# A convolution's first products as two half-width column tiles, copied by one instruction each

## The chip, the cores and the metric

The kernel runs on one core of a Trainium2 chip. The metric is the device time of one execution in microseconds; several executions are given by their median. A profiled execution carries a trace: every instruction with its start, its duration and what released it, every transfer, and the clock that TensorE was granted.

The engines are named as in the profile: PE is TensorE's products, PEld its weight loads, DVE is VectorE, ACT is ScalarE, POOL is GpSimd, and SP issues transfers.

## The reference

The program is a chain of three layers. `x` has 4 batches of 5696 rows and 128 columns, all in fp32.

```python
# layer 1: a causal convolution along the sequence, by FFT of twice the length
Xf = np.fft.rfft(x, n=2*S, axis=1); Hf = np.fft.rfft(h, n=2*S, axis=0)
y = np.fft.irfft(Xf * Hf[None], n=2*S, axis=1)[:, :S]
# layer 2: 8 experts, each takes N/8 rows in the order of their logits, relu(x @ w1) @ w2
# layer 3: 8 experts, each row goes to its best one, times its softmax weight
```

The change is in layer 1 alone. Layers 2 and 3 need all of its output.

## The kernel before, in words

**The convolution as small products.** The sequence of 5696 is 89 x 64. A transform along the 89 is a product with a fixed matrix `F` of 89 x 178 (89 cosines and 89 sines, padded to 96 rows), a transform along the 64 uses one 128 x 128 matrix `EE` per frequency, and the way back uses the transposes and a matrix `G`. All of it is in fp32, and a product of fp32 operands stands in the trace as two weight loads and two passes.

**The first products (`s1`, lines 77 to 94).** The input of one batch lies as 96 partitions (the 89, padded) by 128 `d` by 64. `s1` fetches it in four pieces `g` of 32 `d` into a ring of four buffers `XB` (line 81, issued by SP) and works a piece in four groups `q` of 8 `d`. In a group, each of four products takes the data of two `d` (96 x 128) as weights and streams `F`: the result has 128 partitions, the 64 of the first `d` above the 64 of the second, and 178 columns, cosines ahead of sines. The four results fill 356 columns in each of two banks of a PSUM tile; there are four such tiles, of two banks each, and they are all of PSUM.

The convolution wants something else in SBUF: `A` of 128 partitions (64 cosine, 64 sine) by 89 frequencies by 256 columns, of which one holds one `d` of one batch. So four copies follow, each of 64 partitions and 356 elements: for the first and the second `d` of the pairs, the cosines by ACT and the sines by DVE (line 93). The frequency is the innermost of what a copy writes, with a step of 1 KB between its elements.

**What stands around it.** `s1` runs five times. First for the filter `h`; then for batch 0 in turn with `s2h`, which takes the filter through its second transform (line 106), copies it (line 108) and stores it to `Hd` in DRAM (line 109); one group of `s1` goes with two steps of `s2h`. Then for batch 1. The second transform of these two batches (`s2`, from line 125) needs all of `A` and begins after the last copy; `s3` (line 161) ends the pair and hands rows to the routing. Then `s1` runs for batches 2 and 3, with a step of the routing's search (`head.step`: lines 337 to 406, among them two-column products in line 346) after each group, and `s2` and `s3` follow for that pair. Each stage is in the same instruction streams as the ones around it, in the order that the program gives.

**The order and its limits.** Every engine works its instructions in order. A product needs its piece of `XB` and a free PSUM tile; a copy needs its products; a tile is free when its copies have read it. SP issues the loads of `XB` in order too: a load waits for the products that read the buffer before, and behind the last pieces of `x` stand the matrices `EE` (line 118) and the stored filter (line 122) that `s2` needs.

Of the kernel before, what the change touches and what calls it, by code (L numbers as in the profile page):

```python
# [17 lines left out]
AF = mybir.ActivationFunctionType  # L18
# [30 lines left out]
def conv(tc,nc,a,yrow,LG,head):  # L49

    ctx=contextlib.ExitStack()
    with ctx:
# [6 lines left out]
        F=cp.tile([96,178],F32,name="F"); nc.sync.dma_start(F,a['F'])  # L59
# [5 lines left out]
        A=cp.tile([128,89,256],F32,name="A")  # L65
# [6 lines left out]
        def buf():  # L72
            nx[0]+=1; return XB[nx[0]%4]
        def work(nm): return wk.tile([128,1024],F32,name=nm)
        def apart(i,mine,other):
            tc.declare_no_dep(i.ins,group=other,reason='other columns of A'); tc.add_to_no_dep_group(mine,i.ins)
        def s1(src,col,free=False):

            for g in range(4):
                xt=buf()[:96].rearrange("p (d n) -> p d n",n=64); cuts=(0,8,32) if col==128 and not g else (0,32)  # L80
                for d0,d1 in zip(cuts,cuts[1:]): nc.sync.dma_start(xt[:,d0:d1],src[:,g*2048+d0*64:g*2048+d1*64].rearrange("p (d n) -> p d n",n=64))
                for q in range(4):
                    p=ps.tile([128,2,512],F32,name="ps")
                    for i in range(4):
                        nc.tensor.matmul(p[:,i//2,(i%2)*178:(i%2)*178+178], xt[:,q*8+2*i:q*8+2*i+2,:], F, start=True,stop=True)
                    pv=p[:,:,:356].rearrange("p u (v c k) -> p c u v k",v=2,c=2)
                    for d2 in range(2):
                        for c in range(2):
                            c0=col+g*32+q*8+d2
                            o=A[c*64:(c+1)*64,:,:]  # L90
                            o=o[:,:,c0:c0+7:2].rearrange("p k (u v) -> p u v k",u=2)
                            i=pv[d2*64:(d2+1)*64,c]
                            w=nc.scalar.activation(o,i,AF.Copy) if c==0 else nc.vector.tensor_copy(o,i)  # L93
                            if free: apart(w,'x0','h')
                    yield
        def s2h(col):

# [98 lines left out]
        for i,_ in enumerate(s1(a['hl'],128)):  # L196
            if i==3: later()
        together(s2h(128),s1(a['xl'][0],0,True),2)
        for _ in s1(a['xl'][1],128): pass
        s2(0,head.step); s3(0,head.step)  # L200
# [834 lines left out]
```

## Time and profile before

| | |
|---|---|
| median of three executions | 1952.54 us (1951.1 to 1952.9) |
| profiled execution | 1953.31 us, its span 1951.5 us |
| granted clock of TensorE, mean | 0.946 of full speed |
| PE, PEld busy | 88%, 76% of the span |
| DVE, ACT, POOL busy | 70%, 58%, 47% |
| line 85 (first products) | 640 loads and passes, 119.0 us busy |
| line 93 (their copies) | 160 on ACT, 116.3 us; 160 on DVE, 115.4 us |

The span is the time from the first to the last instruction of the trace. A busy share is a mean over the whole span; what a stage is limited by is read from a window of that stage alone. A weight load and the pass before it lie beside each other, so PEld and PE can be busy at the same time, and a pass's duration holds its way through the array: the distance between two starts is what the next one waits. The form `96*128 96x178` of a product is its weights (rows times columns) and what is streamed through them.

### The profile page before, as it was taken

The numbers are of one execution on the slowest core, as the hardware profiler recorded it, in microseconds if no ns is written. First come the engines' busy times: TensorE is split into PE (matmuls) and PEld (weight loads), VectorE is DVE, ScalarE is ACT, GpSimd is POOL, SyncE is SP. The second block draws the span as 40 slices with busy tenths as digits, with TensorE's granted clock in tenths as the row PEclk, the third lists the DMA queues.
The fourth block names the chain that finished last, engine by engine and source line by source line (L and its number), as shares of the span: only waits on it lengthen the run. The fifth ranks groups of instructions, "written<-read, shape, count | busy, mean of one in ns | idle before, by whom it ended". The sixth has DMA issues, their size and how long they took to land.

```text
span 1951.5 us, 30858 instructions
## 1 busy us (share of the span) xinstructions
PE 1726.4 (88%) x10012; PEld 1491.5 (76%) x10012; DVE 1360.8 (70%) x3416; ACT 1132.9 (58%) x2267; POOL 921.6 (47%) x1058
## 2 busy tenths in 40 slices
PE   6888689777796498999999998999999999999997
PEld 6766589766595387777777777888788888888997
DVE  5588624888546687878888885566876666666885
ACT  5577512877423366566567565556555555566885
POOL 0215411034212446656767767735544444445885
PEclk8989989989898698999999999999999999999998
DMA  8869888369783222212312311103232223233673
GB/s 243 236 176 307 276 237 220 104 183 303 227 231 99 67 54 55 82 42 73 93 56 69 93 51 45 45 21 129 80 115 92 90 88 108 85 108 126 196 212 91
DMA packets 121561, 254.15 MB, mean 130 GB/s; under 512 B 32857, under 2 KB 68576, under 8 KB 119760
## 3 DMA queue, kind: packets, MB, share of 16 engines
q1 hardware_dynamic: 65664, 172.06, 30.1%
q0 software_dynamic: 23024, 50.90, 9.2%
q10 hardware_dynamic: 32704, 29.14, 4.8%
q8 instruction: 81, 1.33, 0.3%
q14 instruction: 88, 0.72, 0.1%
HBM read 178.76 MB, written 74.17 MB: 130 GB/s over the span
## 4 chain that ended last, share of the span: by engine, by line
PE 51%; DVE 8%; DMA 3%; issue 2%; POOL 2%; ACT 1%; DVEq 0%; SPq 0%; POOLq 0%; ACTq 0%
PE ph L634 8%; PE py L648 7%; PE ph L636 7%; PE ph L635 7%; PE py L646 7%; PE py L647 7%; PE tr L625 2%; PE tr L686 2%; DVE hl L639 2%; POOL BK L723 1%; PE rt L913 1%; DVE M L440 1%; DMA xg<-yrow,idx 1%; DMA VT<-Vd 1%; DMA Vd<-V 1%
## 5 line engine op out<-in xcount | busy, mean ns | idle before, releaser
L639 DVE SCALAR_TENSOR_TENSOR hl<-ph,hh 128x480 fp32r<-128x480 f32 (+3 forms) x856 | 522.2, 614 | 247.2 <-ACT hh L638 241.1
L638 ACT ACTIVATE hh<-ph 128x480 fp32r<-128x480 f32 (+3 forms) x856 | 459.5, 542 | 369.4 <-PE ph L636 352.6
L648 PE MATMUL py<-hl,w2h 128*128 128x480 f32 (+3 forms) x856 | 319.3, 373 | 17.3 <-DVE hl L639 16.7
L634 PE MATMUL ph<-xh,w1h 128*128 128x480 f32 (+3 forms) x856 | 330.0, 386 | 0.0
L646 PE MATMUL py<-hh,w2h 128*128 128x480 f32 (+3 forms) x856 | 322.3, 376 | 1.7 <-ACT hh L638 1.7
L636 PE MATMUL ph<-xl,w1h 128*128 128x480 f32 (+3 forms) x856 | 315.2, 369 | 0.0
L635 PE MATMUL ph<-xh,w1l 128*128 128x480 f32 (+3 forms) x856 | 314.8, 368 | 0.0
L647 PE MATMUL py<-hh,w2l 128*128 128x480 f32 (+3 forms) x856 | 312.3, 365 | 0.0
L918 POOL DMA_INDIRECT out_dram<-OR,ids x192 | 196.6, 1024 | 166.9 <-DVE OR L916 112.9
L723 POOL DMA_INDIRECT BK<-RB,pi x192 | 189.0, 984 | 64.6 <-issue 51.9
L741 POOL DMA_INDIRECT xg<-yrow,idx x192 | 187.2, 975 | 68.1 <-issue 48.6
L136 POOL TENSOR_TENSOR m<-m,xs 128x1024 f32<-128x1024 f32 (+2 forms) x46 | 104.0, 2262 | 223.5 <-DVE xs L133 190.7
L648 PEld LDWEIGHTS py<-hl,w2h 128*128 128x128 f32 x856 | 162.3, 190 | 47.3 <-DVE hl L639 24.3
L636 PEld LDWEIGHTS ph<-xl,w1h 128*128 128x128 f32 x856 | 162.9, 190 | 22.4 <-issue 0.2
L646 PEld LDWEIGHTS py<-hh,w2h 128*128 128x128 f32 x856 | 162.7, 190 | 21.4 <-ACT hh L638 2.2
L647 PEld LDWEIGHTS py<-hh,w2l 128*128 128x128 f32 x856 | 163.0, 190 | 19.5
L635 PEld LDWEIGHTS ph<-xh,w1l 128*128 128x128 f32 x856 | 163.6, 191 | 17.6
L634 PEld LDWEIGHTS ph<-xh,w1h 128*128 128x128 f32 x856 | 163.4, 191 | 16.5 <-ACT xh L627 0.5
L599 POOL TENSOR_TENSOR w2l<-w2r,w2h 128x512 fp32r<-128x512 f32 x104 | 133.0, 1298 | 90.5 <-ACT w2h L598 90.4
L161 PE MATMUL ps<-G,XB 96*128 96x128 f32 x1024 | 127.0, 283 | 20.5 <-DMA XB<-Z 20.5
L93 DVE COPY A<-ps 64x356 f32<-64x356 f32 x160 | 115.4, 758 | 38.7 <-ACT A L93 36.0
L93 ACT ACTIVATE A<-ps 64x356 f32<-64x356 f32 x160 | 116.3, 779 | 44.5 <-DVE A L93 19.9
(338 smaller groups left out, 2990.7 us busy)
## 6 DMA issues: line engine op xcount, KB each, us to landing
w1r<-in_moe_w_dram SPq DMA_DIRECT2D x52, 512.0 KB, 3.8
w2r<-in_moe_w2t_dram SPq DMA_DIRECT2D x52, 512.0 KB, 4.1
XB<-Z SPq DMA_DIRECT2D x64, 384.0 KB, 5.2
hh<-Hd SPq DMA_DIRECT2D x88, 256.0 KB, 4.9
XB<-in_EE_dram SPq DMA_DIRECT2D x22, 1024.0 KB, 8.1
Z<-A ACTq DMA_DIRECT2D x44, 512.0 KB, 5.2
XB<-in_xl_dram SPq DMA_DIRECT2D x14, 768.0 KB, 7.0
xg<-BK SPq DMA_DIRECT2D x37, 260.0 KB, 2.8
```

Of the source, the lines that this page charges most:

```text
L93: w=nc.scalar.activation(o,i,AF.Copy) if c==0 else nc.vector.tensor_copy(o,i)
L634: nc.tensor.matmul(ph[:,:N],w1h[:,fs],xh[:,:N],start=True,stop=False)
L635: nc.tensor.matmul(ph[:,:N],w1l[:,fs],xh[:,:N],start=False,stop=False)
L636: nc.tensor.matmul(ph[:,:N],w1h[:,fs],xl[:,:N],start=False,stop=True)
L638: nc.scalar.activation(hh[:,:N],ph[:,:N],AF.Relu)
L639: LD[0]=nc.vector.scalar_tensor_tensor(hl[:,:N],ph[:,:N],0.0,hh.bitcast(F32)[:,:N],op0=ALU.max,op1=ALU.subtract)
L646: nc.tensor.matmul(py[:,:N],w2h[:,fs],hh[:,:N],start=f==0,stop=False)
L647: nc.tensor.matmul(py[:,:N],w2l[:,fs],hh[:,:N],start=False,stop=False)
L648: nc.tensor.matmul(py[:,:N],w2h[:,fs],hl[:,:N],start=False,stop=f==7)
L723: s=nc.gpsimd.indirect_dma_start(out=BK[:,:],out_offset=bass.IndirectOffsetOnAxis(ap=pi[:k,b:b+1],axis=0),in_=RB[:k,b,:W1],in_offset=None)
L741: nc.gpsimd.indirect_dma_start(out=xg[:m,b,:],out_offset=None,in_=yrow[:,:],in_offset=bass.IndirectOffsetOnAxis(ap=idx(i)[:m,4*i+b:4*i+b+1 ...
L918: sc=nc.gpsimd.indirect_dma_start(out=out[:,:],out_offset=bass.IndirectOffsetOnAxis(ap=ids[:,b:b+1],axis=0),in_=OR[:,b,:],in_offset=None,b ...
```

## The change

Each `d` now has two sets of products of its own. The data of one `d` (96 x 64) is loaded as the weights of the left half of the array's columns, with the 89 cosine columns of `F` streamed, and once more as the weights of the right half, with the 89 sine columns. The first writes the PSUM partitions 0 to 63, the second 64 to 127, so a group leaves its results as `A` wants them: cosine above sine. One bank of the PSUM tile then holds four `d`, and one copy of 128 partitions and 356 elements takes it to `A`: the first bank by ACT, with the frequency innermost as before, the second by DVE, with the four columns innermost.

```diff
--- before.py
+++ after.py
@@ -81,17 +81,15 @@
                 for d0,d1 in zip(cuts,cuts[1:]): nc.sync.dma_start(xt[:,d0:d1],src[:,g*2048+d0*64:g*2048+d1*64].rearrange("p (d n) -> p d n",n=64))
                 for q in range(4):
                     p=ps.tile([128,2,512],F32,name="ps")
-                    for i in range(4):
-                        nc.tensor.matmul(p[:,i//2,(i%2)*178:(i%2)*178+178], xt[:,q*8+2*i:q*8+2*i+2,:], F, start=True,stop=True)
-                    pv=p[:,:,:356].rearrange("p u (v c k) -> p c u v k",v=2,c=2)
-                    for d2 in range(2):
+                    for i in range(8):
                         for c in range(2):
-                            c0=col+g*32+q*8+d2
-                            o=A[c*64:(c+1)*64,:,:]
-                            o=o[:,:,c0:c0+7:2].rearrange("p k (u v) -> p u v k",u=2)
-                            i=pv[d2*64:(d2+1)*64,c]
-                            w=nc.scalar.activation(o,i,AF.Copy) if c==0 else nc.vector.tensor_copy(o,i)
-                            if free: apart(w,'x0','h')
+                            nc.tensor.matmul(p[c*64:c*64+64,i//4,(i%4)*89:(i%4)*89+89], xt[:,q*8+i,:], F[:,c*89:c*89+89], start=True,stop=True)
+                    for u in range(2):
+                        c0=col+g*32+q*8+4*u
+                        o=A[:,:,c0:c0+4]
+                        i=p[:,u,:356].rearrange("p (v k) -> p v k",v=4)
+                        w=nc.scalar.activation(o.rearrange("p k v -> p v k"),i,AF.Copy) if u==0 else nc.vector.tensor_copy(o,i.rearrange("p v k -> p k v"))
+                        if free: apart(w,'x0','h')
                     yield
         def s2h(col):
```

## Rows read from the trace of the kernel before

**Rows 1.** The page, part 1: busy us of each engine, share of the span, instructions.

```profile
PE 1726.4 (88%) x10012; PEld 1491.5 (76%) x10012; DVE 1360.8 (70%) x3416; ACT 1132.9 (58%) x2267; POOL 921.6 (47%) x1058
```

**Rows 2.** Windows, by stage: us, busy us (instructions) per engine, granted clock, DMA share, GB/s.

```profile
4.70:42.80 38.10, 27.48 (x136) 25.95 (x137) 23.82 (x36) 25.51 (x35) 0.00 (x0) 0.94 1.00 285
42.80:91.80 49.00, 40.72 (x266) 39.42 (x267) 23.09 (x32) 21.19 (x31) 13.50 (x22) 0.87 0.74 212
91.80:125.40 33.60, 26.30 (x164) 24.11 (x162) 29.31 (x43) 29.34 (x43) 1.00 (x2) 0.97 0.80 228
...
333.30:399.80 66.50, 49.96 (x269) 46.07 (x269) 53.94 (x106) 50.71 (x75) 1.30 (x2) 0.87 0.41 125
```

**Rows 3.** The same windows, instructions of line 85 alone: PE, PEld, clock, DMA, GB/s.

```profile
4.70:42.80 38.10, 27.48 (x136) 25.93 (x136) 0.94 1.00 285
42.80:91.80 49.00, 17.43 (x88) 15.78 (x89) 0.87 0.74 212
91.80:125.40 33.60, 26.21 (x161) 24.05 (x160) 0.97 0.80 228
333.30:399.80 66.50, 47.89 (x256) 44.35 (x256) 0.87 0.41 125
```

**Rows 4.** Groups by line, 97.6 to 125.4 us: busy us, mean ns | idle before.

```profile
L93 DVE COPY A<-ps 64x356 f32<-64x356 f32 x37 | 25.4, 755 | 2.4 <-ACT A L93 2.1
L93 ACT ACTIVATE A<-ps 64x356 f32<-64x356 f32 x36 | 24.9, 783 | 2.2 <-DVE A L93 2.0
L85 PE MATMUL ps<-F,XB 96*128 96x178 f32 x128 | 21.2, 319 | 3.4 <-PE ps L85 1.8 <-DVE A L93 1.6
```

**Rows 5.** Timeline, 118 to 126 us: start us, us, what, count [idle before <-releaser].

```profile
118.80 2.41 PEld L85 LDWEIGHTS ps<-F,XB 96*128 96x128 f32 x16 [0.64 <-PE ps L85]
118.83 2.65 PE L85 MATMUL ps<-F,XB 96*128 96x178 f32 x16 [0.40 <-DVE A L93]
120.14 2.77 ACT L93 ACTIVATE A<-ps 64x356 f32<-64x356 f32 x4 [0.22 <-DVE A L93]
...
123.13 1.35 ACT L93 ACTIVATE A<-ps 64x356 f32<-64x356 f32 x2 [0.22 <-DVE A L93]
...
125.37 1.19 PE L125 MATMUL ps<-A,XB 128*128 128x256 f32 x2 [3.89 <-issue]
```

**Rows 6.** Timeline of PE, 85 to 99 us: a block that waits for nothing.

```profile
91.86 4.99 PE L85 MATMUL ps<-F,XB 96*128 96x178 f32 x32
```

**Rows 7.** Line 85 by itself: duration in ns, min/median/max, first and last start.

```profile
L85 PEld LDWEIGHTS ps<-F,XB x640: 186/190/338, 4.7 to 394.2; 96*128 96x128 f32 x160
L85 PE MATMUL ps<-F,XB x640: 312/314/665, 4.8 to 394.4; 96*128 96x178 f32 x160
```

**Rows 8.** Groups by line and shape, 0 to 460 us: a straight copy, a two-column load.

```profile
L165 DVE COPY xs<-ps 128x712 f32<-128x712 f32 x16 | 14.4, 900 | 49.2 <-PE ps L161 49.2
...
L399 PEld LDWEIGHTS ps<-Ib,mmh 128*2 128x2 f32 x1 | 0.1, 84 | 0.0
```

**Rows 9.** Timeline of PEld, 393.5 to 399.9 us: two loads of a two-column product.

```profile
395.21 0.19 PEld L346 LDWEIGHTS ps<-sg,blkr 128*128 128x128 f32 x1 [0.80 <-PE ps L85]
395.32 0.19 PEld L346 LDWEIGHTS ps<-sg,nblkr 128*128 128x128 f32 x1
```

**Rows 10.** Timeline of PEld, 300.95 to 304.4 us: loads of 128-column products in a row.

```profile
300.90 3.66 PEld L161 LDWEIGHTS ps<-G,XB 96*128 96x128 f32 x32
```

**Rows 11.** Timeline, 4 to 7.5 us: the first group of line 85.

```profile
4.74 2.28 PEld L85 LDWEIGHTS ps<-F,XB 96*128 96x128 f32 x8 [4.74 <-issue]
4.77 2.71 PE L85 MATMUL ps<-F,XB 96*128 96x178 f32 x8 [4.77 <-DMA XB<-in_hl_dram]
```

**Rows 12.** Timeline of PE, 42 to 47 us: the first products of line 106.

```profile
42.81 3.75 PE L106 MATMUL ps<-A,m 128*128 128x128 f32 x16 [3.47 <-issue]
```

**Rows 13.** Waits, 42.8 to 91.8 us: who waited for whom, us, times, longest.

```profile
DVE hh L108 <- DMA Hd<-hh: 12.3, 5, 4.1
...
ACT hh L108 <- DMA Hd<-hh: 5.1, 2, 4.7
```

## The prediction

> **What bounds the kernel now.** I read the page's busy shares first: PE is busy 88% of the span [rows 1], but that is a mean over stages with different limits, so the next view is the windows by stage. The changed code runs in four stretches, and a window restricted to line 85 shows how much of it each holds: 8 passes of line 85 make one group `q` (4 products, and every fp32 product stands in the trace as two weight loads and two passes), so the 640 passes are 80 groups, 17 of them before 42.8 us, 11 between 42.8 and 91.8, 20 between 91.8 and 125.4, and 32 between 333.3 and 399.8 [rows 2, 3]. Everything after 399.8 us waits, in a chain, for the last of them.
>
> The third stretch shows the limit undisturbed. Its groups by line, from its 5.8th microsecond on [rows 4], give the two copy engines 27.8 us in which they copy for 25 us each and mostly wait for one another, and PE waits for PSUM that they hold. In the timeline [rows 5] the reader is to see a rhythm of two groups: 16 passes in 2.65 us, a gap, the next block; ACT starts a run of copies at 120.14 and the next at 123.13, two groups in 2.99 us, 1.50 us per group. PE alone could go faster: 32 passes that wait for nothing take 4.99 us [rows 6], and less the 0.31 us of the last one [rows 7], that is 4.68 / 31 = 151 ns a pass, 1.21 us per group. So the copies bound this stretch, by 0.3 us a group, and the change halves their number. What decides is whether PE, the next limit, stays at 1.21.
>
> **The change part by part.** *The copies.* Four copies of 64 x 356 (two on ACT, two on DVE, each reading both banks) become one of 128 x 356 on each engine, each from its own bank. ACT's keeps its order (the 1 KB step of A innermost), so I price it at the 0.78 us of line 93. DVE's runs four neighbouring columns of A innermost and steps through PSUM, which no row shows; below, the 712-element straight copy of line 165 at 900 ns gives 356/712 of it, 0.45 us; above, two of today's copies, 1.51 us [rows 4, 8]. I take today's 0.76, the nearest row in size. Copying then costs 0.8 us a group, both engines in parallel, against 1.50. Under any PE pace below, this is hidden; it would matter above 1.2 us and only if PE stays at 1.21. The end of each stretch gains: today the first product of the following stage starts 3.9 us after the last pass of line 85 has ended (121.48 to 125.37 [rows 5]); afterwards one copy and a handover follow, 1.2 us.
>
> *The products.* A group goes from 4 products of 128 x 178 to 16 of 64 x 89, that is from 8 passes to 32, with twice the streamed columns in total and, in weight loads, 32 x 64 columns for 8 x 128. Price of a pass of 89 columns: half of 151, 75.5 ns. Price of a weight load of 64 columns: 128 columns follow each other at 112 ns where nothing else binds (395.21 to 395.32) or where 32 loads take 3.66 us ((3.66 - 0.19) / 31) [rows 9, 10]; a load of 2 columns lasts 84 ns against 190 for 128 [rows 7, 8], so each column is 0.84 ns and 64 columns fewer take 54 ns off 112: 58 ns.
>
> How the two combine is what the trace does not show, because it has no product that fills only half of the columns. Bounds: 32 passes one after another, 32 x 75.5 = 2.42 us a group; or the two halves of the array fully side by side, 1.21 us. What the trace does show is when a load starts: the last load of a block of 16 begins at 118.80 + 2.41 - 0.19 = 121.02 and the last pass at 118.83 + 2.65 - 0.31 = 121.17, so the load begins one pass ahead, when the pass before it begins, and not earlier [rows 5, 7]. The program's order per `d` is cosine half twice, sine half twice. If the halves may overlap and each load still waits for the pass before it to begin, a pass on the same half follows after 75.5 ns, a pass on the other half after its 58 ns load: (75.5 + 58) / 2 = 67 ns, 32 of them 2.14 us a group. I take this: it keeps the one rule that the rows show and lies between the ends. PE then bounds at 2.14 where the copies bounded at 1.50.
>
> [...]
>
> *By stretch*, with 2.14 us a group. (1) The first two groups ran at half pace (8 loads in 2.28 us [rows 11]), so they take 4.3 us each from 4.77; 15 more end at 13.3 + 32.1 = 45.4, where the next stage now starts at 42.8 [rows 12]: **+2.6**. (2) 11 groups x 0.93 = 10.2 more PE work, between products of line 106. That stretch has 49.0 - 40.7 = 8.3 us of idle PE [rows 2], and its copies wait for the stores to Hd [rows 13], which PE's longer work can hide behind. I take half, **+5**; 2 and 10 are the ends. (3) 20 x 2.14 + 1.2 = 44.0 for 33.6: **+10.4**. (4) The first group, then 3.5 us until the second (the limits of the search), 31 x 2.14 = 66.3, the half pace of the first two again 4.3, 2 for the search's own products, 1.2 at the end: 77.3 for 66.5, **+10.8**. Loads of x and EE move with PE: each is issued when line 85 frees its buffer, DMA is busy 0.41 of stretch (4) [rows 2], so they stay covered; in (1) DMA is at 1.00 and later use only relieves it. Nothing else is moved or made to wait; behind PE queue only the following products, ACT and DVE do the search's work earlier than today.
>
> Sum: 28.8 us. The profiled execution took 1953.3, the median is 0.8 lower: 1953.3 + 28.8 - 0.8 = **1981 us**. If a load never waits for the pass before it but loads still go one at a time, the pace is 58 ns, 1.86 us a group: 0, +3.6, +4.8, +1.6, together +10, 1962. That is the same mechanism at its lower end.
>
> **The rivals.** *No overlap at all*: the halves run in turn, 2.42 us a group. The four stretches give +7.9, +6.6, +16.0 and 20.0: +50.5, **2003 us**. For it: every pass in the trace starts only when the one before it has streamed. Against it: all those use the same columns.
>
> *The halves run fully side by side* (the faster side): PE stays at 1.21 us a group and the copies no longer bind. It needs loads that run ahead of waiting passes and beside each other, and decides wherever the pace falls below 47 ns a pass (1.50 / 32). Stretch (1) gives back 3 of the 3.9 us of late copies, (2) nothing, since stores bound it, (3) 24.2 + 1.2 = 25.4 for 33.6, -8.2, (4) 3.5 + 37.5 + 2.4 + 2 + 1.2 and 5 for the search's waits = 51.6 for 66.5, -15. Together -26, **1926 us**. [...]
>
> *A load keeps the price of 128 columns*, or does not overlap: 112 ns a pass or more, 3.57 us a group, +23, +21, +39, +51 = +134, **2086 us**. Against it: the load of 2 columns is 106 ns shorter.
>
> **How the numbers follow.** Forecast (58 to 67 ns, 1962 to 1986, the upper end with all 10 of stretch (2)): 0.34. In turn: 0.26. Side by side: 0.28. Dear loads: 0.09. The rest, 0.03, is no change, PE's growth falling into idle time everywhere. Faster by over 0.2% (3.9 us, about what this kernel's measurement can tell from no change): 0.30, slower: 0.65, within: 0.05. The likeliest case's own range is 1962 to 1986. For 8 in 10 the range must take in the faster case too: 1924 to 2006 leaves out the dear loads and the outer tails.
>
> **What would show it.** Line 85's passes: 2,560 of them, starts alternating 58 and 75 ns (forecast), all 75 (in turn), averaging 38 (side by side). Line 93: 80 copies on each engine near 0.78 us, ACT idle with PE as its releaser. The stretch from the first to the last pass of the 32 late groups: 66 us or more by the forecast, 61 before, under 50 if the halves share the array. [...]

## The result, and the profile after

The changed kernel takes **1922.22 us** (median; 1917.37 to 1925.19), the kernel before 1951.82 us (1949.83 to 1952.90) beside it on the same chip: ratio 0.9847, 95% interval 0.9824 to 0.9870. It is faster by 1.5%; the forecast was 1981 us, slower, and its range began at 1924. The rival "the halves run fully side by side" (1926 us) is what happened on PE; that its sum comes so near is partly luck, as the table shows.

Line numbers are smaller by 2 from the copies on: the first products are line 86, their copies line 91, the second stage's products line 104. The page's first part, after (busy us, share of the span, instructions), answers to [rows 1]:

```profile
PE 1724.8 (90%) x11932; PEld 1491.8 (78%) x11932; DVE 1283.3 (67%) x3336; ACT 1079.8 (56%) x2187; POOL 920.8 (48%) x1058
```

PE has 1,920 more passes and is not busier: that alone speaks for side by side. DVE loses 77.5 us and ACT 53.1. The windows of the four stretches, after (columns as in [rows 2]):

```profile
4.70:37.00 32.30, 29.01 (x545) 27.87 (x545) 8.64 (x18) 13.24 (x18) 0.00 (x0) 0.89 1.02 292
37.00:90.80 53.80, 42.52 (x530) 39.09 (x530) 13.24 (x22) 14.45 (x23) 13.94 (x22) 0.90 0.80 224
90.80:123.70 32.90, 25.61 (x642) 24.88 (x641) 11.10 (x21) 16.40 (x22) 0.56 (x1) 1.00 0.76 210
329.20:373.90 44.70, 42.21 (x1038) 41.23 (x1037) 22.84 (x73) 29.42 (x42) 1.19 (x2) 1.00 0.57 164
```

Each stretch begins and ends at the same products as before. From them and [rows 2], in us:

```
stretch                       before   after   change   forecast   side by side
1  first 17 groups              38.1    32.3     -5.8       +2.6           -3
2  11 groups, second stage      49.0    53.8     +4.8       +5              0
3  20 groups, to line 123       33.6    32.9     -0.7      +10.4         -8.2
4  32 late groups               66.5    44.7    -21.8      +10.8          -15
all the rest of the span      1764.3  1758.2     -6.1        0              0
sum                           1951.5  1921.9    -29.6      +28.8        -26
```

The gain stands in stretch 4. The first three together give only 1.7 us, and that is the second thing to explain. (The rest is unchanged code; in the runs below it takes 1749.5 to 1762.8 us with no edit in it, so its 6.1 us are not counted as a gain of the change.) None of the four terms of the side-by-side sum comes within 2 us of its stretch; their errors largely cancel.

The late stretch by groups, after (busy us, mean ns | idle before, releaser):

```profile
L86 PE MATMUL ps<-F,XB 96*64 96x89 f32 x1024 | 40.6, 241 | 0.0
L86 PEld LDWEIGHTS ps<-F,XB 96*64 96x64 f32 x1024 | 39.5, 137 | 0.2
L91 ACT ACTIVATE A<-ps 128x356 f32<-128x356 f32 x32 | 25.3, 791 | 12.3 <-PE ps L86 12.1
L91 DVE COPY A<-ps 128x356 f32<-128x356 f32 x32 | 16.9, 528 | 18.8 <-ACT A L91 18.4 <-DMA XB<-in_xl_dram 0.3
```

The two waits of the same stretch before the change (who <- whom: us, times, longest):

```profile
DVE A L93 <- ACT A L93: 8.9, 15, 1.8
ACT A L93 <- DVE A L93: 8.7, 18, 1.0
```

The reader is to see the roles exchanged: PE has no idle time before its 1,024 passes, ACT waits for PE, and DVE for ACT behind it, where before the two copy engines waited for each other. 1,024 passes in 40.6 us are 39.6 ns each; the median group takes 1.227 us, 38.3 ns a pass. In the trace the starts come in pairs, one pass on each half 6 to 8 ns apart (3 to 17 in stretch 3), a pair every 76.6 ns. That is the prediction's 75.5 ns for a pass of 89 columns, paid once for two. Each load starts some 2 ns behind a pass and lasts 137 ns, so the two loads of a pair lie beside each other too.

Stretch 3 on PE's timeline, after (start us, us, what, count [idle before <-releaser]):

```profile
98.70 5.12 PE L86 MATMUL ps<-F,XB 96*64 96x89 f32 x127 [1.38 <-issue]
106.35 5.13 PE L86 MATMUL ps<-F,XB 96*64 96x89 f32 x128 [2.52 <-issue]
113.45 8.80 PE L86 MATMUL ps<-F,XB 96*64 96x89 f32 x222 [1.97 <-issue]
123.66 0.70 PE L123 MATMUL ps<-A,XB 128*128 128x256 f32 x2 [1.42 <-DVE A L91]
```

Blocks of 127 and 128 passes run at full pace, (5.13 - 0.24) / 127 = 38.5 ns, and between them PE stops with nothing that releases it: 5.9 us in three gaps. A pass is two instructions, so the gaps stand 256 instructions apart. The waits of stretch 2, after (who <- whom: us, times, longest), answer to [rows 13]:

```profile
DVE hh L106 <- DMA Hd<-hh: 20.5, 5, 8.2
...
PEld ps L86 <- DVE hh L106: 9.2, 3, 5.3
PE ps L86 <- DVE hh L106: 8.7, 3, 5.2
```

The wait for the stores to Hd grew from 12.3 to 20.5 us, and now PE's first products stand behind it.

### The profile page after: what moved, and what is told of

It is laid out like the page before. It is cut to its first block, busy times and chain, and to the rows that moved or that the text cites. A ratio compares the mean times of both kernels' runs of the same rounds, so it can differ in the third digit from the quotient of the medians.

```text
span 1921.9 us, 34501 instructions
## 1 busy us (share of the span) xinstructions
PE 1724.8 (90%) x11932; PEld 1491.8 (78%) x11932; DVE 1283.3 (67%) x3336; ACT 1079.8 (56%) x2187; POOL 920.8 (48%) x1058
## 4 chain that ended last, share of the span: by engine, by line
PE 53%; DVE 8%; POOL 2%; issue 2%; DMA 2%; ACT 1%; DVEq 0%; POOLq 0%; ACTq 0%; SPq 0%
PE ph L632 8%; PE py L646 8%; PE ph L634 8%; PE ph L633 8%; PE py L644 8%; PE py L645 8%; PE tr L623 2%; PE tr L684 2%; DVE hl L637 2%; POOL BK L721 1%; PE rt L911 1%; DVE M L438 1%; DMA xg<-yrow,idx 1%; PE rt L556 1%; POOL xg L739 1%
## 5 line engine op out<-in xcount | busy, mean ns | idle before, releaser
L159 PEld LDWEIGHTS ps<-G,XB 96*128 96x128 f32 x1024 | 123.3, 199 | 21.1 <-issue 19.6
L86 PE MATMUL ps<-F,XB 96*64 96x89 f32 x2560 | 112.8, 251 | 22.3 <-DVE hh L106 8.7
```

The source lines that it names most:

```text
L159: nc.tensor.matmul(py[:,j*2+b],Bt[:,c,j,b*128:b*128+128],G[:,c],start=c==0,stop=c==1)
```

## The experiments

Each kernel is compared with runs of the kernel before on the same chip. Theory: two passes on different halves of the columns share the array, so PE stays at 1.21 us a group and the copies stop binding. Rival: the gain is the copies' alone and the halves cost PE something. The edits are shown shortened, that of experiment 1 against the kernel before, all others against the changed one.

**1. The copies alone.** Products as before, at full width; copies as in the change.

```
-  4 copies of 64 x 356 (u, c, d2)
+  for u in range(2): one copy of 128 x 356 from p[:,u,:356] to A[:,:,c0:c0+4]
```

> The products of before (4 of 128 x 178) with the copies of the change (two of 128 x 356). The arrangement of A is wrong in it, so only the convolution's part of the time, up to the first product of the last second transform, is compared. If the half-width products cost nothing against the full-width ones, as the pairs of starts 6 ns apart in the changed kernel say, the stretch of the 32 late groups takes the 44.7 us of the changed kernel, within 1 us, and the copies' halving is the whole gain. If half-width products still cost something (loads twice as many, pairs that do not quite meet), this kernel is shorter there by over 2 us.

1905.21 us, ratio 0.9787 (0.9745 to 0.9828); `A` is arranged otherwise in it, so only its stretches are compared. Windows of line 85 alone, stretches 1 to 4 (us; PE, PEld, clock, DMA share, GB/s):

```profile
4.10:33.00 28.90, 25.61 (x136) 24.59 (x136) 1.00 1.01 298
33.00:85.10 52.10, 17.39 (x89) 14.81 (x90) 0.90 0.86 244
85.10:110.80 25.70, 24.29 (x160) 24.02 (x160) 1.00 0.99 242
317.40:363.30 45.90, 42.71 (x256) 41.28 (x256) 0.93 0.53 157
```

A quarter of the passes gives nearly the same late stretch, 45.9 for 44.7 us: 1.2 us longer, which is neither of the two expectations. Its clock was lower (0.93 for 1.00): three groups near its start took 2.54, 2.37 and 1.54 us, where an undisturbed one takes 1.207. Without these 2.8 us it would have taken some 43.1, an estimate, so the half-width passes cost little there, some 1.6 us: 1.227 for 1.207 us a group, and 1.64 for 1.35 us for the groups in which a round of the search falls. But stretch 3 takes 25.7 us where the change takes 32.9, and none of PE's gaps without a releaser is in it: what the change loses in stretch 3 comes with the number of its instructions.

**2. The products alone.** Half-width products; four copies of 64 partitions.

```
-  for u: one copy of 128 x 356
+  for u: for c in range(2): one copy of 64 x 356 (c=0 on ACT, c=1 on DVE)
```

> The half-width products of the change with four copies of 64 x 356 per group, as many as before, cosines by ACT and sines by DVE. If the copies made the gain, they bind again at 1.2 to 1.5 us a group, the 32 late groups take 55 to 66 us and the total is 1940 to 1952. [...]

1963.8 us, ratio 1.0087 (1.0057 to 1.0117): slower than before, and than expected. Its stretch 3 by waits:

```profile
DVE A L92 <- ACT A L92: 14.0, 19, 0.9
ACT A L92 <- DVE A L92: 13.2, 18, 0.9
```

and two windows inside it (columns as above, all engines):

```profile
110.00:120.00 10.00, 8.66 (x176) 7.99 (x172) 7.14 (x11) 7.21 (x12) 0.00 (x0) 0.88 0.69 196
120.00:130.00 10.00, 8.68 (x136) 8.57 (x138) 7.23 (x12) 7.05 (x11) 0.00 (x0) 0.66 0.42 133
```

The two copy engines wait for each other again, so the gain needs the copies. They wait longer than before the change: in stretch 3 each of them starts a copy every 1.01 us where it was 0.77, that is 2.03 us a group for 1.55, although one copy lasts as long as before (764 ns on DVE and 794 on ACT; 755 and 783 in [rows 4]). So these four copies are dearer than those of before, and the run is no clean copy of the old limit; why their waits are longer stays open. The profiled span is 18.9 us longer than before, and stretches 1 and 3 hold it (47.3 and 43.5 us for 38.1 and 33.6). In stretch 1, 8.8 us are a single wait of DVE for a load of constants (`ck`), a wait of 2.5 us before the change and 1.0 after it; PE stands for 10.5 us meanwhile.

In the second window the granted clock is 0.66: PE gets through 136 passes, while it is busy as long as with 176 at 0.88; before it, PE had been idle for 1.3 of 10 us. The mean of that window lies between 1.00 and 0.50, the two levels that the trace of the change shows (31 to 37 us and 23 to 25 us). Each copy engine gets through 11 or 12 copies in either window, so the clock did not set the pace here. Why it was lower than before the change (0.97 in stretch 3 [rows 2]) stays open.

**3 to 5. How far may the two halves stand apart in the program?** The order of the 32 passes is changed to runs of 16, 4 and 8 passes on one half before the other follows (two passes make one product).

```
-  for i in range(8):
-      for c in range(2): matmul(half c, input i)
+  for c in range(2):                       # runs of 16
+      for i in range(8): ...
+  for i2 in range(0,8,2): c,i = (0,i2),(0,i2+1),(1,i2),(1,i2+1)      # runs of 4
+  for i4 in (0,4): c,i = (0,i4..i4+3),(1,i4..i4+3)                   # runs of 8
```

> The changed kernel with the products of a group in another order: all 16 passes on the left half, then all 16 on the right. If products start in program order and only neighbours on different halves overlap, the passes of a run follow each other at 76.6 ns and only the ends of two runs meet: 30 x 76.6 = 2.30 us a group, and by the sums of the forecast's rival without overlap the total is 1990 to 2003. If each half works its own queue, or products pass one another, the group stays at 1.23 us and the total at 1922.

> The same in runs of four passes on a half. Starts in program order with only neighbours overlapping: 6 x 76.6 ns for 8 passes, 57.5 ns a pass, 1.84 us a group, a total of 1950 to 1965. A queue per half: 1.23 us a group, 1922.

> The changed kernel in runs of 8 passes on a half. If a pass on the other half may start ahead of waiting ones by a fixed reach, which the runs of 16 give as (16 x 76.6 - 977) / 76.6 = 3.2 passes per switch, a group takes 4 x (8 - 3.2) x 76.6 ns = 1.47 us, and the late stretch, 44.7 in the changed kernel, about 52. If the halves have queues of their own and the runs of 16 were slow for another reason, 1.23 us.

Runs of 16: 1949.13 us, ratio 1.0026 (1.0009 to 1.0044), 1.953 us a group, neither 2.30 nor 1.23. Slices of 0.1 us in its late stretch, line 86 alone, show what happens at a change of halves (slice, us, PE busy (passes that run in it), PEld, clock, DMA share, GB/s):

```profile
360.10:360.20 0.10, 0.10 (x4) 0.10 (x3) 1.00 0.47 82
360.20:360.30 0.10, 0.10 (x6) 0.10 (x5) 1.00 0.44 82
...
360.50:360.60 0.10, 0.10 (x8) 0.10 (x4) 1.00 0.00 0
360.60:360.70 0.10, 0.10 (x6) 0.10 (x3) 1.00 0.39 164
360.70:360.80 0.10, 0.10 (x4) 0.10 (x3) 1.00 0.86 328
```

For some 0.5 us more passes run at once, up to twice as many as in the middle of a run: passes of the new half start while the last ones of the old half still have to. The single starts form two trains: 360.214, 360.290, 360.367, 360.444 us, and 360.220, 360.347, 360.424, 360.501 us. The second train begins ahead of three passes of the first. A group in turn would be 32 x 76.6 = 2.45 us; two changes of halves save 0.50, so each saves 0.25 us, 3.2 passes. That fixed reach is what the run of 8 was to test. Its four changes should save 1.0 us and give 1.45 (1.47 and a late stretch of about 52 us were expected); it took 1.453 us a group (late stretch 53.4 us; 1926.69 us, ratio 0.9910, 0.9885 to 0.9934). Runs of 4 lie within the reach: 1.227 us a group, as in the change; 1918.48 us, ratio 0.9854 (0.9813 to 0.9895). The idea that only neighbours in the program overlap (1.84 us) fell there.

**6. More buffers for the stores.** The copies that go to Hd get six buffers of their own in place of three shared ones.

```
-  hs=work("hh")                                  # 3 buffers of the name hh
+  hs=wk.tile([128,512],F32,name="hs",bufs=6)
```

> The changed kernel, with the copies of the filter's second transform in six buffers of their own instead of three shared ones. If the second stretch (53.8 us, 49.0 before) is held by the time one store to Hd takes to land, it shrinks to 45 to 49 and the total by up to 5. If the transfers of that stretch are bound by their bytes, it stays at 52 to 55 and the total at 1922.

1907.36 us (1904.81 to 1912.8), ratio 0.9808 (0.9789 to 0.9828). Its stretch 2 (all engines):

```profile
35.80:80.80 45.00, 40.54 (x530) 37.51 (x530) 12.45 (x21) 13.94 (x22) 13.19 (x21) 0.92 1.02 302
```

and the wait in it that answers to the first of those shown for the change:

```profile
DVE hs L106 <- DMA Hd<-hs: 3.5, 2, 2.3
```

Stretch 2 falls from 53.8 to 45.0 us, DVE's wait for the stores from 20.5 to 3.5, and DMA's share rises from 0.80 to 1.02. So stretch 2 was held by the landing of three buffers' stores. In the runs with three buffers it takes 49.0 to 57.5 us, in the two with six 45.0 and 46.4. This explains the +4.8: stretches 1 and 2 together take 87.1 us before, 86.1 after and 75.3 here. What stretch 1 gained, the stores took back. Up to 5 us in all were expected. The profiled span is 18.9 us shorter than that of the change: 8.8 in stretch 2, 2.0 and 3.0 in stretches 1 and 3, and 7.9 in code that no edit touches, while the late stretch is 2.8 us longer (47.5 us, at a granted clock of 0.93).

**7. More DMA traffic in the late stretch**, to see whether the gaps of stretch 3 follow the traffic. After each late group an extra load of 288 KB, into two buffers, held back by a small DVE copy from the group's result.

```
+  nc.vector.tensor_copy(JK[j%2][:,:1],A[:96,0,c:c+1]); nc.gpsimd.dma_start(JK[j%2], 288 KB of xl)
```

> The changed kernel with an extra load of 288 KB after each of the 32 late groups, whose data nobody reads. If the gaps of the third stretch, one per 256 instructions of PE, are waits for the next block of its instructions, which comes late where other transfers fill the DMA engines, then the same gaps of 0.5 to 3 us appear in the late stretch at the same multiples of 256, eight of them, and it grows from 44.7 to 50 to 60. If the gaps of the third stretch were the pieces of x or PSUM, none appear at those places, and what the extra loads cost shows as a wait for XB.

1956.02 us, ratio 1.0047 (1.0031 to 1.0064), late stretch 76.2 us: a miss, and for another reason than either theory's. DVE's waits from 328 to 404 us:

```profile
DVE JK L203 <- DMA JK<-in_xl_dram: 48.0, 22, 5.1
```

The small copy had to wait until its buffer's last load had landed, and the group's copy stood behind it on DVE. PE has one stop of 2.5 us without a releaser there, but with DVE as the limit that shows little of the gaps; experiment 9 repeats it with so many buffers that hardly anything waits.

**8. ACT's copy in DVE's order.** The change lets ACT step through A by 1 KB and DVE write four neighbouring columns first; here both do the latter.

```
-  nc.scalar.activation(o.rearrange("p k v -> p v k"), i)
+  nc.scalar.activation(o, i.rearrange("p v k -> p k v"))
```

> The changed kernel with ACT's copy in the order of DVE's, four neighbouring columns of A innermost. If that order is what makes DVE's copy 0.53 us where it was 0.76, ACT's goes from 0.79 to about 0.5. Its time is hidden behind PE in either case: the total stays within 3 us of the changed kernel, with 0.3 us less at the end of each stretch.

1913.52 us, ratio 0.9828 (0.9808 to 0.9849). Its late stretch by groups:

```profile
L91 DVE COPY A<-ps 128x356 f32<-128x356 f32 x32 | 16.9, 527 | 17.1 <-ACT A L91 17.1
L91 ACT ACTIVATE A<-ps 128x356 f32<-128x356 f32 x32 | 14.8, 464 | 20.9 <-PE ps L86 20.9
```

ACT's copy goes from 791 to 464 ns and the stretch stays as it was (44.4 for 44.7 us): ACT's idle time takes it up, since PE binds. The interval overlaps that of the change, so no gain in all is shown.

**9. Experiment 7 again, in eleven buffers of 192 KB**, so that DVE need not wait for a landing.

```
+  nc.vector.tensor_copy(JK[j%11][:,:1],A[:96,0,c:c+1]); nc.gpsimd.dma_start(JK[j%11], 192 KB of xl)
```

> An extra load of 192 KB is issued after each of the 32 late groups, into eleven buffers of its own so that nothing waits for it (about 160 GB/s on top of the 164 GB/s of that stretch). Theory (PE's instructions come in blocks of 256 that share the DMA engines, and a block that is fetched while the engines are busy arrives after PE needs it): gaps of 0.3 to 3 us that nothing releases appear in the late stretch at PE instructions that stand 194 behind a multiple of 256, where the changed kernel has none; 8 blocks fall into it, so the stretch of 44.7 us becomes 47 to 58. Rival (the gaps of the third stretch belong to that stretch, not to the traffic): no such gap, 44 to 46 us.

One run, 1929.67 us. DVE waits for landings for 2.8 us in all, where it was 48. The late stretch (all engines), and PE's timeline in it:

```profile
324.90:374.80 49.90, 43.37 (x1037) 41.67 (x1036) 26.92 (x104) 29.61 (x42) 17.17 (x33) 0.99 0.96 258
```

```profile
353.12 1.60 PE L86 MATMUL ps<-F,XB 96*64 96x89 f32 x36 [1.48 <-issue]
...
359.47 4.20 PE L86 MATMUL ps<-F,XB 96*64 96x89 f32 x103 [0.84 <-issue]
...
371.47 1.90 PE L86 MATMUL ps<-F,XB 96*64 96x89 f32 x42 [1.52 <-issue]
```

The gaps appear where the change has none, at the places of the 256 instructions, and the stretch takes 49.9 us for 44.7 (47 to 58 was expected); DMA's share is 0.96 there in place of 0.57. Four groups at such places are 5.1 us longer than the others of their kind, which is the whole growth. The queue that carries instructions, in the DMA view of this stretch, first the change and then this kernel (packets, MB, share):

```profile
q8 instruction: 8, 0.13, 1.2%
```

```profile
q8 instruction: 7, 0.11, 1.0%
```

That is 16 KB a packet, one for about 256 instructions (8 for the 1,038 passes and 1,037 loads of the change). A crossing is the start of the first instruction of a new block of 256. The packets' times in the trace against the crossings give the mechanism; these are the first five blocks that begin in the late stretch:

```
                    fetch starts behind the crossing before, us   lands ahead of the next crossing, us
change, late        0.50  0.08  0.34  0.69  0.95                  3.31  3.88  3.75  3.06  3.10
with extra loads    0.39  1.94  3.14  4.02  3.58                  3.43  2.11  1.43  1.39  1.56
```

In the change the next block is fetched 0.08 to 0.95 us after the last one begins. The transfer takes as long in both (0.9 to 1.3 us), but under traffic it starts up to 4 us late, and in neither does PE go on earlier than 1.4 us behind the landing. At 38.3 ns a pass a block lasts about 5 us, so by estimate a start later than some 2.4 us (5 - 1.2 - 1.4) stops PE. The three gaps of the change's stretch 3 fit this: the fetches start 3.9, 5.1 and 4.3 us behind their crossings, and PE goes on 1.4 us behind each landing. Where DMA is less busy in stretch 3, the gaps are shorter: 2.0 and 1.5 us in all in experiments 10 and 6, at shares of 0.63 and 0.65. What exactly delays the fetch is not shown.

**10. Both edits, 6 and 8.**

> The changed kernel with both edits that helped alone: the store's copies in six buffers of their own, and ACT's copy also in the order of four neighbouring columns. If the two gains lie in different waits they add: stretch 2 near 45 us as with the six buffers, ACT copies 0.47 us, the late stretch 44 to 47, and 1898 to 1908 us in all. If the faster copy only moves the wait to the stores again, as fast as the six buffers alone, 1907.

1912.07 us (1905.69 to 1920.04), ratio 0.9829 (0.9796 to 0.9861): the second of the two expectations, if either; no gain over the six buffers alone is shown. Stretch 2 takes 46.4 us and the late stretch 47.5, of which these two windows (all engines) are the first two thirds:

```profile
313.20:330.00 16.80, 15.75 (x307) 15.29 (x308) 6.79 (x26) 4.93 (x11) 1.22 (x2) 0.80 0.45 114
330.00:345.00 15.00, 15.00 (x376) 14.76 (x374) 7.60 (x23) 6.95 (x16) 0.00 (x0) 1.00 0.56 149
```

The first window ran at a granted clock of 0.80, where the change had 1.00; that is the difference to 44.7. Leaving out experiment 1, which arranges A otherwise, six buffers alone (experiment 6) is the fastest version, 1907.36 us; its interval just touches that of the change, and 8.8 us of the difference stand in the stretch that the edit was made for.

## Why the prediction was wrong, point by point

**The step that failed** is the rule for two halves: "If the halves may overlap and each load still waits for the pass before it to begin, a pass on the same half follows after 75.5 ns, a pass on the other half after its 58 ns load: (75.5 + 58) / 2 = 67 ns". The rule was read from [rows 5, 7], where all loads and passes use the same columns: there the pass before is always one on the same columns, so the rows can't tell "waits for the pass before" from "waits for the pass before on its own half". The runs show the second. A pair starts every 76.6 ns with its passes at most 17 ns apart, which leaves no 58 ns for a load between them. With runs of 16 and 8 a pass goes ahead of up to three older ones of the other half. With 38.3 in place of 67 ns a group takes 1.227 in place of 2.14 us, PE's limit falls below the copies' 1.50, and the sign turns. The rival's own condition for this, "the pace falls below 47 ns a pass", decided, and the sign that the prediction named for it, "under 50 if the halves share the array", came: 43.2 us from the first to the last pass of the late groups. By experiments 3 and 5 the sentence ahead of the prediction that every engine works its instructions in order is too strong for PE.

Two halves take 1.227 us a group where 2.45 (32 x 76.6 ns) would be in turn: 2.0 times the pace, with a fresh load per pass. All of line 86 uses the same 96 rows, and its loads of 137 ns lie beside passes.

**What was right.** The price of a load: 54 ns less than one of 128 columns was predicted, and 190 went to 137. The pass on one half: 75.5 predicted, 76.6 measured. ACT's copy: 0.78 predicted, 0.79 measured. That the copies bound stretches 3 and 4 before: experiments 1 and 2 each change one side, and only the copies move the time down. The end of a stretch: 1.2 us predicted, 1.42 us measured in stretch 3 and 1.14 in stretch 4, before line 123.

**What was off in size.** DVE's copy took 0.53 us, not the 0.76 chosen, within its bounds (0.45 to 1.51); hidden either way. Stretch 4 gained 21.8 us where the rival's sum had 15. Group starts in the trace split it: first to last group 60.0 us before, 41.9 after (-18.1), and 6.5 to 2.9 from there to line 123 (-3.6). The rival priced the rhythm (31 x (1.50 - 1.21) = 9.0) and left 5 us for the search's waits. But before, groups of 2.5 to 4.0 us came back with the search's rounds (2.49, 3.04 and 3.96 us, twice over), and in the timeline the search's small instructions stand there between the copies, on the engines that bound; after, PE binds, and a round costs one group of 1.64 us. No run takes the search out, so this part is read from the timeline alone. Part may be the clock, 0.87 before [rows 2] and 1.00 after: with 0.80 in the first third the same stretch took 47.5 us in experiment 10. Of the sums, that of the dear loads (2,086 us) leaves out the half pace of the first two groups and takes 21 us for stretch 2 where the others take half of the added work; in their way it gives +30, +13, +39 and +58, or 2,092 us. Nothing hangs on it.

**What gave the gain back.** Stretch 1 gained 5.8, and stretch 2 lost 4.8 to the stores, which the forecast had at +5 for another reason (PE's work), a hit by luck, and the rival at 0; experiment 6 shows the three buffers as the cause. In stretch 3 the rival's 25.4 us would have come true with the products of before (25.7 in experiment 1). The half-width products bring four times the passes, a block of instructions lasts 5 us in place of about 19 (128 x 151 ns), and where DMA is busy (0.76 of stretch 3) the blocks come late: 5.9 of the 7.2 us. Experiment 1 has no such stop at a share of 0.99. No view that I priced held the fetch of PE's instructions, and "32 passes for 8" was counted in columns alone.

## What to carry to other kernels

A rule for when a load or a pass may start, read from instructions that all use the same part of the array, says nothing about instructions on disjoint parts: give "they share it fully" the weight that the missing row deserves, and interleave the halves within four passes if you want it (1.227 us a group here in runs of two and of four, 1.453 in runs of eight). Before splitting products into smaller ones, divide the 256 instructions that one packet brought here by the instructions per us on PE, which gives the time that a block lasts (5 us here), and look at how busy DMA is in that stretch (0.76 and 0.96 where PE stopped). And look at what else stands on the engine that binds: freeing it pays for that work too.

## What the runs showed of the hardware that was not expected

- Passes on two halves of the columns, each with its own load, start 38.3 ns apart on average; at a change of halves three passes start ahead of older ones of the other half, by the pace 3.2 (1.953, 1.453 and 1.227 us a group with runs of 16, 8 and 4).
- One packet of 16 KB came on the instruction queue for about every 256 instructions of PE (8 for 2,075 in the late stretch of the change); with DMA busy (0.76 and 0.96) it came late and PE stood for 0.8 to 2.5 us.
- The same 356 elements of 128 partitions from PSUM cost 791 ns on ACT with a 1 KB step innermost and 464 ns with four neighbouring columns innermost; on DVE the latter took 528 ns, and 758 ns on 64 partitions with the step.
